# Zero matmuls moved to the front, memory rows copied by DMA, a different reuse order of two PSUM banks and function tables loaded by name, in an attention and MoE kernel

## The chip, the cores and the metric

The kernel runs on one core of a Trainium2 chip. The metric is the device time in microseconds (us) of one execution. Three executions of the kernel before were timed; their median is 242.94 us (241.69 to 244.8). A further execution was profiled, and the views quoted here are of that one.

The engines go by the names of the profile: PE multiplies matrices (PEld is its weight load), DVE and ACT are the vector and scalar engines, POOL is GpSimd, SP issues transfers. POOL and SP each have a queue of transfers.

## The reference

Chunked attention with a few memory rows, then a two-layer MLP with a sine-based activation. Inputs are float32: q, k and v of (4, 8, 768, 64), memory keys and values of (4, 8, 8, 64), `w_in` of (512, 2048), `w_out` of (2048, 512), `alpha` of (2048).

```python
chunk, left_ctx, right_ctx = (32, 16, 8)
for c in range(nc):
    l_start, r_end = max(0, c*32 - 16), min(S, c*32 + 32 + 8)
    k_full = concatenate([mem_k, k[:, :, l_start:r_end]])     # 8 memory rows first
    v_full = concatenate([mem_v, v[:, :, l_start:r_end]])
    a = softmax(q_chunk @ k_full.T / sqrt(D))
    out[chunk] = a @ v_full
x = out as (3072 tokens, 512)
h = x @ w_in
g = h + sin(alpha * h)**2 / alpha
result = g @ w_out
```

## The kernel before, in words

The four batches (768 tokens each) go through attention one after the other, and each then through the MLP. All data is cast to bfloat16 on its way in, and PE adds up in float32 in PSUM. The order of the instructions on each engine is the order in which the Python code issues them; nothing is reordered.

**Attention.** A batch is cut into 8 query blocks of 96 rows (`NJ`, `QW`). A block's keys are 128 wide: the context and, in the middle, the 8 memory rows. For the first batch the work goes by pairs of heads (`attention_first`): `turn` (L214) transposes k and q of a pair of heads on PE, `put_k` (L226) and `put_q` (L239) copy them out of PSUM on ACT and DVE, `unit_scores` (L309) multiplies and exponentiates, `unit_values` (L334) multiplies with the values tile `vw` and divides by the sum, and `unit_turn` (L354) transposes the result into `xT`. For the later batches `scores` (L249), `values` (L274) and `turn_x` (L294) do the same for each block. Keys and queries of batches 2 and 3 are gathered as rows into `kst` and `qst` by DMAs on POOL's queue (`load_rows`, L134) and transposed by DMAs on SP's queue (`cross`, L156).

**Memory rows.** The 8 memory values of a batch have to stand in partitions 64 to 71 of `vw`, once for each head and block: `put_memv` (L180) copies them there from the chip tile `memv_st`, on DVE for batches 0 and 1 and on POOL for batches 2 and 3. The memory keys of batches 2 and 3 are copied by POOL into `kst` in `load_rows` (L147); those of batches 0 and 1 are transposed by PE (L545) and put in their place by DVE (`put_memk`, L186).

**MLP.** `layer` (L575) goes over 16 tiles of the hidden width. For each, `first` (L456) does 8 matmuls (L442) into one of three or four two-bank pieces of PSUM, ACT takes the sine (L462), ACT, DVE or POOL squares it (L466, L469), and DVE adds h and writes `gT` (L472), which frees the PSUM piece. The second matmul (`second`, L479) is a generator: one call of it gives one matmul (L485) with 512 columns. Its 6 times 16 matmuls are fed in between the work of the next batch's attention and next layer (`feed.take`). After each 16 the result is copied to `o_sb` (L494 on DVE or L496 on ACT, by turns) and stored from SP's queue.

**The two single banks.** Banks 6 and 7 (ring `one`) are shared by `second`, which keeps one for 16 matmuls, and by `turn_x`, which uses the other for a few transposes. `take_bank` (L87) gives the first bank of the ring that nobody keeps and moves it to the ring's end.

**The start.** PE multiplies zeros (`warm`, L304, tile `idle`) in a few places where it would otherwise wait. ACT's table of functions is loaded when the kernel goes over from `Exp` to `Sin` or back; `preload_act_table` does it where the code says, otherwise it happens just ahead of the first instruction that needs the other table.

Of the kernel before, what the change touches and what calls it, by code (L numbers as in the profile page):

```python
# [15 lines left out]
ACTF = mybir.ActivationFunctionType  # L16
# [26 lines left out]
def kernel(  # L43
# [90 lines left out]
    def load_rows(b):  # L134
        for j in range(NJ):
            lo = QW * j - 16
            r0 = max(0, -lo)
            nc.gpsimd.dma_start(  # L138
                kst[r0:64, j, :].rearrange("p (h d) -> p h d", d=D),
                k[b, :, lo + r0:lo + 64, :].rearrange("h p d -> p h d"),  # L140
            )
            n = min(56, S - (QW * j + 48))
            nc.gpsimd.dma_start(  # L143
                kst[72:72 + n, j, :].rearrange("p (h d) -> p h d", d=D),
                k[b, :, QW * j + 48:QW * j + 48 + n, :].rearrange("h p d -> p h d"),
            )
        nc.gpsimd.tensor_copy(  # L147
            kst[64:72], memk_st[64:72, b - 2, :].unsqueeze(1).to_broadcast([NM, NJ, H * D])
        )
        for t in range(NSUB):  # L150
            nc.gpsimd.dma_start(  # L151
                qst[:, t, :].rearrange("p (h d) -> p h d", d=D),
                q[b, :, P * t:P * t + P, :].rearrange("h p d -> p h d"),
            )
# [25 lines left out]
    def put_memv(b, eng, h0, h1):  # L180
        eng.tensor_copy(  # L181
            vws[b % 2][64:72, h0:h1, :, 0:D],
            memv_st[64:72, b, h0:h1, :].unsqueeze(2).to_broadcast([NM, h1 - h0, NJ, D]),
        )

    def put_memk(b):  # L186
        nc.vector.tensor_copy(
# [166 lines left out]
    def unit_turn(xT, hp, half, x_blk):  # L354
# [7 lines left out]
        )  # L362

    def attention_first(kq, early, ahead):
        xT = xp.tile([P, KT, S], BF, name="xT")
        pt, xb = {}, {}

        def turns(hp):
            put_k(0, hp, turn(kq[0], hp, None))
            put_q(0, hp, turn(kq[1], hp, None))  # L370

        def sc(hp):
            for half in range(2):
                pt[hp, half] = unit_scores(hp, half)

        def pv(*u):
            xb[u] = unit_values(*u, pt[u])

        def x(*u):
            unit_turn(xT, *u, xb.pop(u))  # L380

        warm(12)
        turns(0)
        warm(1)
        turns(1)
        sc(0)
        turns(2)
        sc(1)
        turns(3)
        sc(2)  # L390
        sc(3)
        nc.scalar.preload_act_table(ACTF.Sin)
        early()
        warm(10)
        plan(big=rings["t"][0:1] + rings["big"])
        pv(0, 0)
        pv(0, 1)
        warm(1)
        x(0, 0)
        pv(1, 0)  # L400
        warm(1)
        x(0, 1)
        pv(1, 1)
        warm(1)
        x(1, 0)
        warm(4)
        x(1, 1)
        pv(2, 0)
        pv(3, 0)
        warm(1)  # L410
        x(2, 0)
        pv(2, 1)
        warm(1)
        x(3, 0)
        pv(3, 1)
        ahead(0, 0, xT)
        x(2, 1)
        ahead(1, 0, xT)
        x(3, 1)
        ahead(2, 0, xT)  # L420
        return xT

    def attention(b, stream, shares, lag):
        xT = xp.tile([P, KT, S], BF, name="xT")
        ptl, xbl = {}, {}
        for s in range(NJ + lag + 1):
            n = shares[s] if s < len(shares) else 0
            if s < NJ:
                ptl[s] = scores(b, s)
            stream.take(n // 2)  # L430
            if 0 <= s - lag < NJ:
                xbl[s - lag] = values(b, s - lag, ptl.pop(s - lag))
            stream.take(n - n // 2)
            if 0 <= s - lag - 1 < NJ:
                turn_x(xT, s - lag - 1, xbl.pop(s - lag - 1))
        return xT
# [42 lines left out]
    def second(i, gT):  # L479
        for s in range(NSUB):  # L480
            bank = take_bank("one")
            kept.add(bank)
            o = ps[:, bank, :]
            for ft in range(FT):
                nc.tensor.matmul(  # L485
                    o, gT[:, ft, P * s:P * s + P], w_out_sb[:, ft, :],
                    start=(ft == 0), stop=(ft == FT - 1),
                )
                if ft < FT - 1:
                    yield  # L490
            kept.remove(bank)
            o_sb = mlp.tile([P, d_model], F32, name="o_sb", bufs=2)
            if s % 2 == 0:
                nc.vector.tensor_copy(o_sb[:], o)  # L494
            else:
                nc.scalar.copy(o_sb[:], o)  # L496
            nc.sync.dma_start(out[S * i + P * s:S * i + P * s + P, :], o_sb[:])
            yield
# [7 lines left out]
        nc.sync.dma_start(memk_f[NM * bb:NM * bb + NM], mem_k[bb].rearrange("h n d -> n h d"))  # L506
    nc.sync.dma_start(alpha_rows[:], moe_alpha.rearrange("(ft p) -> ft p", p=P))
    nc.vector.memset(idle[:], 0.0)
    for vw in vws:
        nc.vector.memset(vw[0:32, 0, 0, 0:D], 0.0)  # L510
        nc.vector.memset(vw[96:128, H - 1, NJ - 1, 0:D], 0.0)
# [28 lines left out]
    nc.vector.tensor_copy(biasb[:, 0, 0, 0:1], biasm[:, 3:4])  # L540
    nc.vector.tensor_copy(biasb[:, 1, 3, 2:3], biasm[:, 4:5])
    nc.vector.tensor_copy(memk_bf[:], memk_f[0:32])
    mt = packed(single(), HP, 32)
    for g in range(HP):
        nc.tensor.transpose(mt[:, g, :], memk_bf[0:32, 2 * g:2 * g + 2, :].rearrange("p e d -> p (e d)"), ident[0:32, 0:32])  # L545
    nc.vector.tensor_copy(memkT[:], mt)
    put_memk(0)
    nc.vector.tensor_copy(ident_f[:], ident[0:FT, 0:FT])
    for pt in pts:
        nc.vector.memset(pt[:, H * QW:H * QW + 32], 0.0)  # L550
# [5 lines left out]
    def early():  # L556
        at = single()[:, 0:FT]
        nc.tensor.transpose(at, alpha_rows[:], ident_f[:])
        nc.vector.tensor_copy(alpha_sb[:], at)
        nc.vector.reciprocal(inv_alpha[:], alpha_sb[:])  # L560
        put_memv(0, nc.vector, 0, H)
        put_memv(1, nc.vector, 0, H)

    feed = Feed()
    xT = attention_first(kq, early, ahead)
# [39 lines left out]
    for bb in range(2):  # L605
        nc.gpsimd.dma_start(memk_st[64:72].rearrange("n b (h d) -> n b h d", d=D)[:, bb],
                            mem_k[2 + bb].rearrange("h n d -> n h d"))
    feed.take(8)
    prs = [pair_up(kq1[n % 2], n // 2) for n in range(3)]
    for pc in range(2 * HP):  # L610
# [2 lines left out]
        if pc + 3 < 2 * HP:  # L613
            prs.append(pair_up(kq1[(pc + 3) % 2], (pc + 3) // 2))
        feed.take(2)
    put_memk(1)
    load_rows(2)
    xT = attention(1, feed, (6, 4, 4, 3, 3, 3, 3, 3, 3, 3, 3), 2)
    load_v(2, 0, H)
    put_memv(2, nc.gpsimd, 0, H)  # L620

    for i in range(1, B):
        last = i == B - 1

        def begin(ft, i=i):
            if ft == 2 and i + 1 < B:
                cross(i + 1)

        plan(h=rings["big"])
        layer(i, xT, "AAAV", begin, feed.left() - (0 if last else 16))  # L630
        if not last:
            if i + 2 < B:
                load_rows(i + 2)
            plan(big=rings["h"])
            xT = attention(i + 1, feed, (10, 8, 4, 4, 3, 3, 3, 3, 4, 4, 4), 2)
            if i + 2 < B:
                load_v(i + 2, 0, H)
                put_memv(i + 2, nc.gpsimd, 0, H)
    feed.take(200)


# [28 lines left out]
```

## Time and profile before

| | us |
|---|---|
| median of three executions | 242.94 |
| the profiled execution's own time | 242.81 |
| its span, first to last instruction | 241.0 |
| PE busy | 212.7 |
| ACT busy | 153.2 |
| DVE busy | 141.7 |
| POOL busy | 96.2 |

The profiled execution's time lies within 0.13 us of the median; 1.8 us of it lie outside the span. The stages by time in the span: start and first attention to about 34, first layer to about 57, second attention to about 83, second layer to about 110, third attention to about 131, third layer to about 161, fourth attention to about 181, fourth layer to about 215, and then PE alone with the rest of the last second matmul.

In the timeline, a row gives the start, the busy time, engine, line and operation, and in brackets how long the engine had been idle before it and what ended that. In the view of waits, a row gives who waited for whom, the total in us, how often, and the longest.

### The profile page before, as it was taken

Reading aid. Unit: us, or ns where it says so; the run is one execution under the profiler, and the core shown is the slowest. Engines: PE = TensorE matmul, PEld = TensorE weight load, DVE = VectorE, ACT = ScalarE, POOL = GpSimd, SP = SyncE. Lnnn points to the kernel's source line nnn. Section 1 sums busy time; section 2 is a strip of 40 time slices with the busy share of each in tenths; the row PEclk is TensorE's granted clock in tenths of the full one; section 3 lists DMA queues with packets and bytes.
Section 4 is the critical chain, followed back from the end, with each engine's and each line's share of the span. In section 5 each row is a group of like instructions: output and inputs, shape, how many; then the busy total and the mean of one; then the engine's idle time right before and its main releaser. Section 6 shows DMA issues by size and latency. Waiting matters only on the chain.

```text
span 241.0 us, 4411 instructions
## 1 busy us (share of the span) xinstructions
PE 212.7 (88%) x1707; PEld 117.0 (49%) x1733; DVE 141.7 (59%) x246; ACT 153.2 (64%) x224; POOL 96.2 (40%) x106
## 2 busy tenths in 40 slices
PE   0989787898989997999778999999789899999993
PEld 0454454555445554554445555554455455554441
DVE  5155756898828648778675476645673646663110
ACT  2069349689387497899663977898647577680000
POOL 8867603497999992599991000000000000000000
PEclk9999999999999999999999999999999999999998
DMA  6999999999999999999999954302001101102212
GB/s 89 166 122 121 205 207 207 204 139 89 78 94 117 115 124 131 128 175 149 189 125 136 133 109 88 109 3 87 31 15 46 44 0 44 45 4 87 87 44 87
DMA packets 90646, 25.14 MB, mean 104 GB/s; under 512 B 78833, under 2 KB 87553, under 8 KB 90625
## 3 DMA queue, kind: packets, MB, share of 16 engines
q0 software_dynamic: 71616, 14.82, 110.7%
q1 hardware_dynamic: 19008, 10.04, 20.3%
q8 instruction: 13, 0.21, 0.4%
q14 instruction: 9, 0.07, 0.1%
HBM read 29.67 MB, written 6.29 MB: 149 GB/s over the span
## 4 chain that ended last, share of the span: by engine, by line
PE 64%; DVE 15%; ACT 9%; issue 9%; POOL 1%; DVEq 0%; ACTq 0%; POOLq 0%
PE ps L485 28%; PE ps L442 24%; DVE gT L472 5%; ACT u L462 4%; PE ps L254 3%; DVE u L469 3%; PE ps L307 2%; PE ps L280 2%; ACT u L466 2%; DVE o_sb L494 1%; PE ps L297 1%; PE ps L218 1%; DVE x_blk L347 1%; DVE qT L240 1%; DVE vw L181 1%
## 5 line engine op out<-in xcount | busy, mean ns | idle before, releaser
L485 PE MATMUL ps<-w_out_sb,gT 128*128 128x512 bf16 x360 | 96.8, 379 | 4.1 <-ACT o_sb L496 1.4
L442 PE MATMUL ps<-xT,w_in_sb 128*128 128x384 bf16 x512 | 92.3, 326 | 5.0 <-DVE gT L472 4.8
L472 DVE SCALAR_TENSOR_TENSOR gT<-u,inv_alpha,ps 128x768 bf16<-128x768 f32 x64 | 63.7, 1012 | 34.9 <-ACT u L466 33.8
L462 ACT ACTIVATE u<-ps,alpha_sb 128x768 f32<-128x768 f32 x64 | 57.1, 898 | 24.1 <-PE ps L442 23.3
L442 PEld LDWEIGHTS <-w_in_sb 128*128 128x128 bf16 x512 | 49.6, 98 | 43.9 <-issue 8.7
L485 PEld LDWEIGHTS <-gT 128*128 128x128 bf16 x384 | 34.3, 98 | 31.5 <-issue 2.6
L466 ACT ACTIVATE u<-u 128x768 f32<-128x768 f32 x44 | 37.1, 844 | 1.3
L267 ACT ACTIVATE pt<-ps,biasm 128x256 bf16<-128x256 f32 x72 | 28.6, 480 | 9.2 <-PE ps L254 9.0
L496 ACT COPY o_sb<-ps 128x512 f32<-128x512 f32 x12 | 7.0, 586 | 25.2 <-PE ps L485 19.2
L494 DVE COPY o_sb<-ps 128x512 f32<-128x512 f32 x12 | 8.3, 689 | 21.7 <-PE ps L485 21.7
L469 DVE TENSOR_TENSOR u<-u 128x768 f32<-128x768 f32 x16 | 19.7, 1231 | 2.2 <-ACT u L462 2.1
L287 DVE TENSOR_TENSOR x_blk<-ps,rinv 96x512 bf16<-96x512 f32 x24 | 16.5, 686 | 0.8
L228 ACT COPY kT<-ps 128x672 bf16<-128x672 bf16 x8 | 5.7, 717 | 14.1 <-PE ps L221 10.7
L138 POOL DMA_DIRECT2D kst<-in_k_dram x16 | 11.3, 704 | 7.6 <-DMA kT<-kst 7.6
L286 DVE RECIPROCAL rinv<-ps 96x8 f32<-96x8 f32 x24 | 4.9, 202 | 13.4 <-PE ps L280 13.4
L469 POOL TENSOR_TENSOR u<-u 128x768 f32<-128x768 f32 x4 | 6.4, 1606 | 14.8 <-ACT u L462 14.7
L143 POOL DMA_DIRECT2D kst<-in_k_dram x16 | 11.8, 736 | 0.1
L297 PEld LDWEIGHTS <-x_blk 96*128 96x128 bf16 x96 | 6.7, 97 | 8.9 <-issue 3.4
L280 PEld LDWEIGHTS <-pt 128*128 128x128 bf16 x192 | 9.0, 97 | 4.1 <-issue 0.3
L300 DVE COPY xT<-ps 128x384 bf16<-128x384 bf16 x24 | 8.3, 347 | 3.8 <-PE ps L297 3.8
L151 POOL DMA_DIRECT2D qst<-in_q_dram x12 | 10.5, 906 | 0.0
L297 PE MATMUL ps<-ident,x_blk 96*128 96x96 bf16 x96 | 8.0, 205 | 2.6 <-DVE o_sb L494 2.5
(75 smaller groups left out, 175.7 us busy)
## 6 DMA issues: line engine op xcount, KB each, us to landing
out_dram<-o_sb SPq DMA_DIRECT2D x24, 256.0 KB, 2.0
vw<-in_v_dram POOLq DMA_DIRECT2D x6, 384.0 KB, 10.7
w_out_sb<-in_moe_w_out_dram POOLq DMA_DIRECT2D x2, 1024.0 KB, 18.2
w_in_sb<-in_moe_w_in_dram POOLq DMA_DIRECT2D x3, 512.0 KB, 12.2
qst<-in_q_dram POOLq DMA_DIRECT2D x12, 128.0 KB, 5.0
kst<-in_k_dram POOLq DMA_DIRECT2D x14, 64.0 KB, 4.3
kst<-in_k_dram POOLq DMA_DIRECT2D x14, 56.0 KB, 4.7
k_bf<-in_k_dram POOLq DMA_DIRECT2D x4, 192.0 KB, 5.7
```

What stands on the lines that cost most here:

```text
L138: nc.gpsimd.dma_start(kst[r0:64, j, :].rearrange("p (h d) -> p h d", d=D), k[b, :, lo + r0:lo + 64, :].rearrange("h p d -> p h d"),)
L143: nc.gpsimd.dma_start(kst[72:72 + n, j, :].rearrange("p (h d) -> p h d", d=D), k[b, :, QW * j + 48:QW * j + 48 + n, :].rearrange("h p d -> ...
L267: nc.scalar.activation(pt[:, 0:H * QW].rearrange("p (g e c) -> p g e c", g=2, e=4)[:, :, :, 32 * m:32 * m + 32], sc[:, :, 0:4 * QW].rearra ...
L280: nc.tensor.matmul(otv[:, e, hp, :], pt[:, QW * i:QW * i + P], vws[b % 2][:, 2 * hp + e, j, 0:D + 1],)
L287: nc.vector.tensor_tensor(out=x_blk[:].rearrange("p g e d -> p e g d"), in0=otv[0:QW, :, :, 0:D], in1=rinv[:].unsqueeze(3).to_broadcast([Q ...
L297: nc.tensor.transpose(xtp[:, kt, :], x_blk[:, kt].rearrange("p e d -> p (e d)"), ident[0:QW, 0:QW])
L442: nc.tensor.matmul(hT[:, hf, 0:HALF], w_in_sb[:, kt, P * ft:P * ft + P], xT[:, kt, HALF * hf:HALF * hf + HALF], start=(kt == 0), stop=(kt ...
L462: nc.scalar.activation(u[:], hT[:, :, 0:HALF], ACTF.Sin, scale=alpha_sb[:, ft:ft + 1])
L466: nc.scalar.activation(u[:], u[:], ACTF.Square)
L469: eng.tensor_tensor(out=u[:], in0=u[:], in1=u[:], op=ALU.mult)
L472: nc.vector.scalar_tensor_tensor(out=gT[:, ft, :].rearrange("p (e c) -> p e c", e=2), in0=u[:], scalar=inv_alpha[:, ft:ft + 1], in1=hT[:, ...
L485: nc.tensor.matmul(o, gT[:, ft, P * s:P * s + P], w_out_sb[:, ft, :], start=(ft == 0), stop=(ft == FT - 1),)
```

## The change

Five edits, whose line numbers in the changed kernel are a little higher.

1. **Start.** 8 zero matmuls are issued right behind the memset of the zeros. The transposes of the first batch's memory keys, with their two DVE copies, move from the front of PE's order to behind the first pair of heads. The 12 zero matmuls ahead of the first pair of heads go; between the first and the second there are 2 instead of 1.
2. **Memory rows.** In `load_rows`, and for the values of batches 1, 2 and 3, the copies on POOL and DVE become DMAs from the chip tiles on SP's queue: one for the keys, and 8 (one for each block) for the values of a batch.
3. **Banks.** When `second` gives up its bank, the bank goes to the end of the ring.
4. **Tables.** The loads are asked for by name: `Sin` behind the last `Exp` of an attention, `Exp` behind the last piece of k of batch 1 and behind each later layer.
5. `put_memk(1)` is issued ahead of the second batch's transposes rather than behind them.

```diff
@@ load_rows
-        nc.gpsimd.tensor_copy(
+        nc.sync.dma_start(
             kst[64:72], memk_st[64:72, b - 2, :].unsqueeze(1).to_broadcast([NM, NJ, H * D])
         )
@@ behind put_memv
+    def send_memv(b):
+        for j in range(NJ):
+            nc.sync.dma_start(vws[b % 2][64:72, :, j, 0:D], memv_st[64:72, b])
@@ attention_first
-        warm(12)
         turns(0)
-        warm(1)
+        mt = packed(single(), HP, 32)
+        for g in range(HP):
+            nc.tensor.transpose(mt[:, g, :], memk_bf[0:32, 2 * g:2 * g + 2, :].rearrange("p e d -> p (e d)"), ident[0:32, 0:32])
+        nc.vector.tensor_copy(memkT[:], mt)
+        put_memk(0)
+        warm(2)
         turns(1)
         sc(0)
@@ attention
                 ptl[s] = scores(b, s)
+            if s == NJ - 1:
+                nc.scalar.preload_act_table(ACTF.Sin)
             stream.take(n // 2)
@@ second
             kept.remove(bank)
+            rings["one"].remove(bank)
+            rings["one"].append(bank)
             o_sb = mlp.tile([P, d_model], F32, name="o_sb", bufs=2)
@@ the start
     nc.vector.memset(idle[:], 0.0)
+    warm(8)
     for vw in vws:
...
     nc.vector.tensor_copy(memk_bf[:], memk_f[0:32])
-    mt = packed(single(), HP, 32)
-    for g in range(HP):
-        nc.tensor.transpose(mt[:, g, :], memk_bf[0:32, 2 * g:2 * g + 2, :].rearrange("p e d -> p (e d)"), ident[0:32, 0:32])
-    nc.vector.tensor_copy(memkT[:], mt)
-    put_memk(0)
     nc.vector.tensor_copy(ident_f[:], ident[0:FT, 0:FT])
@@ early
         put_memv(0, nc.vector, 0, H)
-        put_memv(1, nc.vector, 0, H)
+        send_memv(1)
@@ between the first layer and the second attention
+    put_memk(1)
     feed.take(8)
...
         feed.take(2)
-    put_memk(1)
+        if pc == 2 * HP - 2:
+            nc.scalar.preload_act_table(ACTF.Exp)
     load_rows(2)
     xT = attention(1, feed, (6, 4, 4, 3, 3, 3, 3, 3, 3, 3, 3), 2)
     load_v(2, 0, H)
-    put_memv(2, nc.gpsimd, 0, H)
+    send_memv(2)
@@ the loop over the later batches
             plan(big=rings["h"])
+            nc.scalar.preload_act_table(ACTF.Exp)
             xT = attention(i + 1, feed, (10, 8, 4, 4, 3, 3, 3, 3, 4, 4, 4), 2)
             if i + 2 < B:
                 load_v(i + 2, 0, H)
-                put_memv(i + 2, nc.gpsimd, 0, H)
+                send_memv(i + 2)
```

PE's first instructions, before: `memk_bf` holds the memory keys, `idle` the zeros, `k_bf` the first pair of heads. Repetitions are left out.

```order
L545 LDWEIGHTS memk_bf
L545 MATMUL ps<-ident,memk_bf 128x32
...
L307 LDWEIGHTS idle
L307 MATMUL ps<-idle 128x512
...
L221 LDWEIGHTS k_bf
L221 MATMUL ps<-ident,k_bf 64x128
```

PE's first instructions in the changed kernel, where the zeros are L311, the transposes of k and q L225 and those of the memory keys L389.

```order
L311 LDWEIGHTS idle
L311 MATMUL ps<-idle 128x512
...
L225 LDWEIGHTS k_bf
L225 MATMUL ps<-ident,k_bf 64x128
...
L225 LDWEIGHTS q_bf
L225 MATMUL ps<-ident,q_bf 64x128
...
L389 LDWEIGHTS memk_bf
L389 MATMUL ps<-ident,memk_bf 128x32
```

The zeros now come first and the memory keys behind the first pair of heads.

DVE at the end of the first batch's scores, before and in the changed kernel: `alpha_sb` is what the sine needs, `vw` the values tiles, `rinv` the first step behind the values' matmul.

```order
L559 COPY alpha_sb<-ps 128x16
L560 RECIPROCAL inv_alpha<-alpha_sb 128x16
L181 COPY vw_87<-memv_st 8x64x64
L181 COPY vw_88<-memv_st 8x64x64
L346 RECIPROCAL rinv<-ps 96x8
```

```order
L567 COPY alpha_sb<-ps 128x16
L568 RECIPROCAL inv_alpha<-alpha_sb 128x16
L181 COPY vw_87<-memv_st 8x64x64
L350 RECIPROCAL rinv<-ps 96x8
```

One of the two copies of memory values ahead of the first `rinv` has left DVE.

SP's queue, the difference in its first part: `out_dram` are the stores of results.

```order
-L497 DMA out_dram<-o_sb 128x512 x4
+L188 DMA vw_88<-memv_st 8x8x64 x8
+L509 DMA out_dram<-o_sb 128x512
+L147 DMA kst<-memk_st 8x8x512
+L509 DMA out_dram<-o_sb 128x512 x2
+L188 DMA vw_87<-memv_st 8x8x64 x8
+L509 DMA out_dram<-o_sb 128x512
 L158 DMA_TRANSPOSE kT_83<-kst 128x4x128 x8
```

The transfers of memory rows now stand between the stores and ahead of the transposes of batch 2; POOL's copies L147 and L181 are gone from its order.

## The prediction

> **What bounds the kernel now.** I read the view of PE's waits first, since the table above gives PE as the busiest engine by far, and then the timeline at each place that the waits name. PE's waits, with their totals:
>
> ```profile
> PE ps L545 <- DVE memk_bf L542: 5.9, 1, 5.9
> PE ps L442 <- DVE gT L472: 4.8, 7, 1.6
> PE ps L297 <- DVE o_sb L494: 2.5, 2, 1.2
> ...
> PE ps L485 <- ACT o_sb L496: 1.4, 2, 0.7
> PE ps L254 <- DVE gT L472: 1.4, 1, 1.4
> PE ps L485 <- DVE o_sb L494: 1.3, 2, 0.8
> PE ps L254 <- DVE kT L187: 1.0, 1, 1.0
> ```
>
> The last stage is PE alone and the change does not touch its work. What it can win is in these rows: the start, in which PE stands until the memory keys are there; waits for the copy of a result out of a single bank (2.5, 1.4 and 1.3, together 5.2); and waits for `gT`, of which two have a cause that the change removes. A wait of PE in the middle of the kernel counts in full as long as PE finds other work late too, and between about 67 and 215 us PE rarely waits for anything else.
>
> **The start.** Timeline of the first 30 us:
>
> ```profile
> 0.86 0.27 DVE L508 MEMSET idle<- 128x256 uint32 x1 [0.86 <-PEq L654]
> ...
> 6.07 5.08 PE L307 MATMUL ps<-idle 128*128 128x512 bf16 x12
> ...
> 11.08 0.53 PE L221 MATMUL ps<-ident,k_bf 128*64 128x128 bf16 x12
> ...
> 13.58 0.93 POOL L173 DMA_DIRECT2D vw<-in_v_dram  x1 [0.66 <-DMA q_bf<-in_q_dram]
> ...
> 14.92 1.52 ACT L328 ACTIVATE pt<-ps 128x768 bf16<-128x768 f32 x2 [0.77 <-PE ps L320]
> ...
> 16.33 0.71 ACT L228 COPY kT<-ps 128x672 bf16<-128x672 bf16 x1
> ...
> 17.08 0.32 DVE L234 COPY kT<-ps 128x48 bf16<-128x48 bf16 x2 [1.71 <-ACT kT L228]
> 17.32 0.95 DVE L240 COPY qT<-ps 128x768 bf16<-128x768 bf16 x1
> ...
> 20.87 0.34 PE L320 MATMUL ps<-qT,kT 64*128 64x96 bf16 x8
> 21.58 0.34 PE L320 MATMUL ps<-qT,kT 64*128 64x96 bf16 x8
> ...
> 22.24 2.11 PE L307 MATMUL ps<-idle 128*128 128x512 bf16 x9 [0.16 <-issue]
> 22.61 2.55 DVE L181 COPY vw<-memv_st 8x4096 bf16<-8x4096 bf16 x2
> 24.18 0.67 PE L340 MATMUL ps<-vw,pt 128*128 128x65 bf16 x16
> 25.19 0.20 DVE L346 RECIPROCAL rinv<-ps 96x8 f32<-96x8 f32 x1
> ```
>
> Before, the first pair of heads is transposed at 11.08, behind twelve zero matmuls that began only at 6.07. In the changed kernel the zeros can begin at 1.2 and end by 4.6 (8 by 5.08/12 = 0.42), and the pair is then taken when it lands. I do not credit the 5 us in full, because the transfers end later: POOL's row at 13.58 is a queue slot that came free when the third piece of q had landed, so that piece is there at about 13.5 and no edit makes it earlier. From there the chain is, each step from the rows above: transposes 0.53 (14.1), the second pair's scores, the first half of them 21.58 - 20.87 = 0.71 (14.8), two exponentials 1.52 (16.3), `put_k` of the last pair on ACT 0.71 (17.05), DVE's two small copies until L240 starts 0.24 and L240 0.95 (18.3), L320 of the last pair 0.34 and its second half 0.71 (19.4). Before, that end is 21.58 + 0.34 = 21.9. The start gives 2.5, not 5.
>
> Behind it stand ten zeros and L340, before at 24.18 and now at 21.7. `rinv` then waited until 25.16 for the second of the two copies in the L181 row (2.55 for both); without it, it follows L340 by 0.45, at 22.15. Together 25.19 - 22.15 = **3.0**.
>
> The cover of this is the second half of v, which the later units need:
>
> ```profile
> 16.23 0.68 POOL L178 DMA_DIRECT2D vw<-in_v_dram  x1
> ...
> 29.49 0.67 PE L340 MATMUL ps<-vw,pt 128*128 128x65 bf16 x16
> ```
> ```profile
> vw<-in_v_dram POOLq DMA_DIRECT2D x1, 31.0 KB, 8.8
> ```
>
> It lands at 16.23 + 8.8 = 25.0 and is now needed at 29.49 - 3.0 = 26.5: 1.5 us are left, so the gain passes on.
>
> The zeros serve the clock. Twelve of them ran at 0.42 each, and later ones at 2.11/9 = 0.23, so PE began at half speed and was at full speed for the transposes at 11.08. Eight end earlier than twelve did: whether they suffice no row shows. If not, PE's terms in that chain (0.53 + 0.71 + 0.34 + 0.71 = 2.3) double, until the dense stretch from 13.5 on releases the clock. I put that loss at 1.6; its bounds are 0, and 2.3 + 10 x (0.42 - 0.23) = 4.2 if the ten zeros behind the scores are slow too. The Trainium skill's page "TensorE: Matmul & The Clock Gate", Part 1, says that the clock is released after a busy window of about 3.4 us which runs freely, and its table "Why this matters for your kernels" asks for at least 4 us of work without a pause. By that rule 8 zeros, 3.4 us, would as a rule not fill a window, and it speaks against this edit; the row of twelve agrees, whose 5.08 us passed nearly whole at half speed.
>
> **Memory rows.** POOL's copies, DVE's squares beside them, and PE:
>
> ```profile
> 88.16 3.59 POOL L181 COPY vw<-memv_st 8x4096 bf16<-8x4096 bf16 x1
> ...
> 90.62 1.95 DVE L469 TENSOR_TENSOR u<-u 128x768 f32<-128x768 f32 x1
> ...
> 93.74 2.98 PE L442 MATMUL ps<-xT,w_in_sb 128*128 128x384 bf16 x16 [1.31 <-DVE gT L472]
> ...
> 110.58 3.59 POOL L147 COPY kst<-memk_st 8x4096 bf16<-8x4096 bf16 x1
> ...
> 111.65 3.33 DVE L469 TENSOR_TENSOR u<-u 128x768 f32<-128x768 f32 x1
> ...
> 116.08 0.35 PE L254 MATMUL ps<-qT,kT 64*128 64x96 bf16 x8 [1.35 <-DVE gT L472]
> ```
> ```profile
> L469 DVE TENSOR_TENSOR u<-u x16: 950/958/3329, 40.5 to 216.4; 128x768 f32<-128x768 f32 x16
> ```
>
> A square takes 0.96 (median of 16). The two long ones end with POOL's copy or after it: 88.16 + 3.59 = 91.75, and 110.58 + 3.59 = 114.17. DVE stood still for POOL, 1.0 and 2.4 us, and PE behind it 1.31 and 1.35. With the copies gone PE gets back 1.0 at the first (DVE's own loss bounds it) and 1.35 at the second (PE's wait bounds it): **2.4**, and at most 2.7. That POOL is freed of 14.4 us of copies is worth nothing beside that: no row has PE wait for POOL.
>
> What comes instead: 24 transfers for the values and 2 for the keys, on SP, between stores. SP has no other work, and a store behind them delays only the reuse of `o_sb`, of which there are two, with one result each 7 us or so. The price is in the transfer engines, where the first 8 run beside the loads of v and `w_in`. They are 8 x 8 x 8 = 512 packets of 128 bytes. What a packet costs, from the queues over the first 20 us (q1, SP's) and over the whole span (q0, POOL's):
>
> ```profile
> q1 hardware_dynamic: 320, 0.07, 2.0%
> ```
> ```profile
> q0 software_dynamic: 71616, 14.82, 110.7%
> ```
>
> That is 0.020 x 16 x 20 us / 320 = 20 ns and 1.107 x 16 x 241 us / 71616 = 60 ns: 10 to 31 us of one engine's time. Spread over 8 engines it is 1.3 to 3.8 us on each, on 16 half of that. I take it as hidden by the 1.5 us of slack (20 ns, the same queue); the bound above is 3.8 - 1.5 = 2.3. The Trainium skill's page "DMA: Bandwidth & Descriptors", Rules for kernel authors, says that a slowest dimension below 16 confines a transfer to as many engines; these have 8 partitions, so by it the 8-engine figure holds. No run here shows it yet.
>
> **Banks.** Where PE waits for a bank that was just given up:
>
> ```profile
> 77.38 0.59 PE L485 MATMUL ps<-w_out_sb,gT 128*128 128x512 bf16 x2 [0.54 <-DVE o_sb L494]
> ...
> 122.53 0.68 DVE L494 COPY o_sb<-ps 128x512 f32<-128x512 f32 x1
> ...
> 123.26 0.33 PE L297 MATMUL ps<-ident,x_blk 96*128 96x96 bf16 x4 [1.25 <-DVE o_sb L494]
> ...
> 123.80 0.39 PE L485 MATMUL ps<-w_out_sb,gT 128*128 128x512 bf16 x1
> ...
> 130.19 0.59 PE L485 MATMUL ps<-w_out_sb,gT 128*128 128x512 bf16 x2 [0.72 <-ACT o_sb L496]
> ...
> 190.13 0.38 PE L485 MATMUL ps<-w_out_sb,gT 128*128 128x512 bf16 x1 [0.78 <-DVE o_sb L494]
> ```
>
> The waits view counts those of 1.25 and 0.72 twice (third and fourth attention). In the changed ring the next taker gets the other bank. At 77.38 and 190.13 that one is free: 0.5 and 0.8. At 123.26 `turn_x` gets the free bank at 122.0, but the L485 behind it (123.80) then needs the bank in question at 122.55, whose copy ends at 122.53 + 0.68 = 123.2: 0.7 of the 1.25 comes back, 0.55 is won, twice. At 130.19 the other bank is `turn_x`'s own, read until about 129.7: 0.45 is won, twice. Sum 0.5 + 0.8 + 1.1 + 0.9 = **3.3**, of 5.2 at most.
>
> **The rest.**
>
> ```profile
> 66.72 0.22 DVE L187 COPY kT<-memkT 128x256 bf16<-128x256 bf16 x1
> ```
>
> This copy stands between PE and the second batch's first scores (the wait of 1.0); moved ahead it gives **0.2**, since the copy of q before it stays. The named table loads stand in the same gaps of ACT, where no row has PE wait for a load: nothing. Were one on the path, it would cost its 1.28.
>
> **Sum.** 3.0 + 2.4 + 3.3 + 0.2 = 8.9. The profiled execution took 242.81, the median of the runs is 242.94, so no correction: 242.8 - 8.9 = **233.9**.
>
> **Rivals.**
> - *The zeros don't release the clock.* For it: eight are fewer than the twelve that hardly sufficed; against it: the transposes and scores that follow keep PE busy too. 233.9 + 1.6 = 235.5.
> - *The bank waits only move.* The copy out of the bank takes as long as ever, and there are two banks; if whoever comes second waits in full, the 3.3 goes: 237.2. Against it: at 77.38 and 190.13 the next taker has no one close behind.
> - *The transfers' slack is too short.* At 60 ns a packet on 8 engines the second half of v comes 3.8 later: 233.9 + 2.3 = 236.2.
> - *Slower: the packets queue on one engine.* 31 us there ahead of v's last piece, less 1.5 of slack, stall PE for 29 us: 233.9 + 29 = 263. It makes the kernel slower from 8.9 + 1.5 = 10.4 us on, some 170 packets at 60 ns on one engine. Against it: each of these transfers writes 8 partitions in 64 separate packets, and nothing in the rows of q1 hints at a pile-up.
>
> **Chances.** Forecast 0.50, clock 0.28, banks 0.10, short slack 0.08, slower 0.04. Low end: all 5.2 of the banks and 2.7 of the squares, 233.9 - 1.9 - 0.3 = 231.7, rounded to 231.5 for the start's unknowns. High end: the clock case with its upper bound, 233.9 + 4.2 = 238.1, and the bank case, 237.2; I take 238.0. A measurement of this kernel can tell about 2% from no change, which is 4.9 us or 238.1: all cases but the last lie below it, some of them only by a little. Faster 0.86, within 2% 0.10, slower 0.04.
>
> **What would show it.** The first transposes of k before 7 us and L340's first at about 21.7 would bear out the start; the spacing of L320's halves (0.7 or 1.4) decides on the clock. No square above 1.1 us bears out the memory rows. Bank waits of PE for `o_sb` should sum to about 2, not 5.2. The prediction is wrong if the values' matmul of the later units waits for a transfer, or if layers that were paced by PE turn out to be paced by ACT, so that regained time comes back as another wait.

## The result, and the profile after

| | before | after |
|---|---|---|
| median of four executions, us | 242.45 (241.69 to 244.8) | 233.26 (233.11 to 233.95) |
| the profiled execution, us | 242.81 | 233.11 |
| its span, us | 241.0 | 231.3 |
| PE / DVE / POOL busy, us | 212.7 / 141.7 / 96.2 | 215.7 / 136.4 / 80.8 |

The ratio is 0.9611, with a 95% interval of 0.954 to 0.9681: 9.2 us less, where 8.9 were predicted. All 9.7 us of the span are found by setting the two timelines beside each other at marks that both have (the first `rinv`, PE's first scores and first layer matmul of each batch, and the end of the last layer's matmuls). For the second batch after the change the mark is 63.03, where seven of the first eight scores run behind a wait of 0.65, and not 62.16, where one ran alone:

| stretch | before | after | won |
|---|---|---|---|
| start to the first `rinv` | 25.19 | 20.89 | 4.30 |
| rest of the first attention | 7.07 | 7.07 | 0 |
| first layer and the transposes of the second batch | 34.74 | 35.07 | -0.33 |
| second attention | 15.70 | 15.05 | 0.65 |
| second layer | 27.32 | 26.32 | 1.00 |
| third attention | 20.77 | 18.64 | 2.13 |
| third layer | 30.82 | 30.85 | -0.03 |
| fourth attention | 19.36 | 18.39 | 0.97 |
| fourth layer | 34.26 | 33.35 | 0.91 |
| PE alone to the end | 25.77 | 25.67 | 0.10 |

PE's waits after the change (who waited for whom, total in us, how often, longest):

```profile
PE ps L452 <- DVE gT L482: 3.9, 8, 1.6
PE ps L495 <- DVE o_sb L506: 1.6, 2, 0.8
...
PE ps L311 <- DVE vw L523: 1.2, 1, 1.2
PE ps L258 <- DVE qT L244: 0.7, 1, 0.7
```

The wait of 5.9 for the memory keys is gone and the waits for `o_sb` went from 5.2 to 1.6. The wait of 1.2 at L311 is new, but it is only the time until the first tiles are set, with which the kernel begins.

**The start**, timeline of the changed kernel:

```profile
1.19 3.59 PE L311 MATMUL ps<-idle 128*128 128x512 bf16 x8 [1.19 <-DVE vw L523]
5.23 0.85 PE L225 MATMUL ps<-ident,k_bf 128*64 128x128 bf16 x12 [0.45 <-DMA k_bf<-in_k_dram]
...
8.19 0.85 PE L225 MATMUL ps<-ident,k_bf 128*64 128x128 bf16 x12
...
11.15 0.53 PE L225 MATMUL ps<-ident,k_bf 128*64 128x128 bf16 x12
...
12.06 0.93 POOL L173 DMA_DIRECT2D vw<-in_v_dram  x1 [0.38 <-DMA q_bf<-in_q_dram]
...
14.57 0.53 PE L225 MATMUL ps<-ident,q_bf 128*64 128x128 bf16 x12 [0.35 <-DMA q_bf<-in_q_dram]
...
15.50 0.95 DVE L244 COPY qT<-ps 128x768 bf16<-128x768 bf16 x1
...
18.27 2.33 PE L311 MATMUL ps<-idle 128*128 128x512 bf16 x10
18.87 1.22 DVE L181 COPY vw<-memv_st 8x4096 bf16<-8x4096 bf16 x1
20.44 0.67 PE L344 MATMUL ps<-vw,pt 128*128 128x65 bf16 x16
20.89 0.20 DVE L350 RECIPROCAL rinv<-ps 96x8 f32<-96x8 f32 x1 [0.81 <-PE ps L344]
```

Three things are to be seen. The first pair is transposed at 5.23, before the 7 us that the prediction gave as a sign. It takes 0.85 and not 0.53, so in this execution the eight zeros had not released the clock; the transposes at 11.15 are the first at full speed. And POOL's row that marks the third piece of q stands at 12.06, not 13.58. L344 comes at 20.44, 1.3 earlier than the 21.7 of the prediction.

**The squares**, timeline, and the view of the tile `u` (shortest/median/longest in ns):

```profile
85.99 0.95 DVE L479 TENSOR_TENSOR u<-u 128x768 f32<-128x768 f32 x1
...
88.12 1.46 PE L452 MATMUL ps<-xT,w_in_sb 128*128 128x384 bf16 x8 [0.31 <-DVE gT L482]
...
106.03 0.95 DVE L479 TENSOR_TENSOR u<-u 128x768 f32<-128x768 f32 x1
```
```profile
L479 DVE TENSOR_TENSOR u<-u x16: 950/952/1543, 36.2 to 206.8; 128x768 f32<-128x768 f32 x16
```

Both long squares are back at 0.95. The longest left, 1.54, is the one in the first layer that had that length before as well, beside a square of POOL's.

**The bank**, timeline:

```profile
116.22 0.38 PE L495 MATMUL ps<-w_out_sb,gT 128*128 128x512 bf16 x1 [0.80 <-DVE o_sb L506]
...
165.72 0.38 PE L495 MATMUL ps<-w_out_sb,gT 128*128 128x512 bf16 x1 [0.80 <-DVE o_sb L506]
```

These two are all that is left of PE's waits for `o_sb`: the matmul behind `turn_x` takes the bank whose copy is not yet made.

### The profile page after: what moved, and what is told of

Read it like the earlier page. It is cut to its first block, busy times and chain, and to the rows that moved or that the text cites. A ratio compares the mean times of both kernels' runs of the same rounds, so it can differ in the third digit from the quotient of the medians.

```text
span 231.3 us, 4462 instructions
## 1 busy us (share of the span) xinstructions
PE 215.7 (93%) x1730; PEld 117.5 (51%) x1730; DVE 136.4 (59%) x245; ACT 153.3 (66%) x224; POOL 80.8 (35%) x102
## 4 chain that ended last, share of the span: by engine, by line
PE 67%; DVE 11%; ACT 9%; issue 6%; DMA 3%; POOL 2%; DVEq 0%; ACTq 0%; POOLq 0%
PE ps L495 32%; PE ps L452 25%; ACT u L472 5%; DVE gT L482 4%; DMA q_bf<-in_q_dram 3%; PE ps L258 3%; ACT u L476 2%; PE ps L284 2%; PE ps L301 1%; PE ps L311 1%; DVE x_blk L291 1%; DVE x_blk L351 1%; POOL k_bf L164 1%; PE ps L222 1%; POOL q_bf L164 1%
## 5 line engine op out<-in xcount | busy, mean ns | idle before, releaser
L495 PE MATMUL ps<-w_out_sb,gT 128*128 128x512 bf16 x384 | 102.1, 380 | 2.2 <-DVE o_sb L506 1.6
L479 DVE TENSOR_TENSOR u<-u 128x768 f32<-128x768 f32 x16 | 15.9, 995 | 2.2 <-ACT u L472 2.1
L138 POOL DMA_DIRECT2D kst<-in_k_dram x16 | 11.0, 688 | 12.6 <-DMA kT<-kst 12.6
L143 POOL DMA_DIRECT2D kst<-in_k_dram x16 | 11.5, 719 | 0.5 <-DMA vw<-in_v_dram 0.5
L151 POOL DMA_DIRECT2D qst<-in_q_dram x12 | 10.5, 902 | 2.0 <-DMA qT<-qst 1.5
L311 PE MATMUL ps<-idle 128*128 128x512 bf16 x29 | 9.9, 465 | 1.2 <-DVE vw L523 1.2
```

The costliest lines, as they stand in the source:

```text
L138: nc.gpsimd.dma_start(kst[r0:64, j, :].rearrange("p (h d) -> p h d", d=D), k[b, :, lo + r0:lo + 64, :].rearrange("h p d -> p h d"),)
L143: nc.gpsimd.dma_start(kst[72:72 + n, j, :].rearrange("p (h d) -> p h d", d=D), k[b, :, QW * j + 48:QW * j + 48 + n, :].rearrange("h p d -> ...
L311: nc.tensor.matmul(z, idle[:, 0:P], idle[:])
L479: eng.tensor_tensor(out=u[:], in0=u[:], in1=u[:], op=ALU.mult)
L495: nc.tensor.matmul(o, gT[:, ft, P * s:P * s + P], w_out_sb[:, ft, :], start=(ft == 0), stop=(ft == FT - 1),)
```

## The experiments

Twelve kernels ran, each beside runs of the kernel before on the same chip. Each edit is against the changed kernel.

| run | median, us (range) | ratio to before (95%) |
|---|---|---|
| `e1_start_old` | 236.37 (236.01 to 236.72) | 0.9745 (0.9681 to 0.9809) |
| `e4_pool_rows` | 237.12 (235.49 to 237.8) | 0.9766 (0.9693 to 0.984) |
| `e5_spare_copy` | 235.52 (234.58 to 237.77) | 0.9724 (0.9643 to 0.9804) |
| `e6_banks_old` | 237.72 (235.8 to 238.54) | 0.9776 (0.9685 to 0.9866) |
| `a1_after` | 233.32 (232.13 to 233.79) | 0.9621 (0.9557 to 0.9686) |
| `e2_no_zeros` | 233.4 (232.98 to 235.32) | 0.9648 (0.9576 to 0.9719) |
| `e3_zeros_16` | 233.28 (232.02 to 234.47) | 0.9626 (0.9557 to 0.9696) |
| `e12_memv1_pool` | 233.22 (232.44 to 234.73) | 0.9627 (0.9543 to 0.9711) |
| `e7_memv1_dve` | 233.04 (232.94 to 233.69) | 0.9615 (0.9552 to 0.9677) |
| `e8_tables_memk_old` | 233.29 (232.62 to 234.32) | 0.963 (0.9569 to 0.9691) |
| `e10_swap_evac` | 232.93 (232.5 to 234.86) | 0.9627 (0.9561 to 0.9693) |
| `e15_mid_swap` | 231.78 (231.47 to 232.97) | 0.9583 (0.9548 to 0.9619) |

The first four ran on one chip, the next four on a second, then three on the first again and the last on a third. No unaltered run stands beside the first four, but all their executions (234.58 at least) lie above all eight of the changed kernel (233.95 at most). One execution of a kernel differs from another by 0.7 to 3.5 us, so an effect below 1 us is read from the stretches of the profile, not from the medians.

### The start undone

```diff
-    warm(8)
...
+    mt = packed(single(), HP, 32)
+    for g in range(HP):
+        nc.tensor.transpose(mt[:, g, :], ...)
+    nc.vector.tensor_copy(memkT[:], mt)
+    put_memk(0)
...
+        warm(12)
         turns(0)
-        mt = packed(single(), HP, 32)
...
-        put_memk(0)
-        warm(2)
+        warm(1)
```

> The changed kernel with the old start: twelve zero matmuls behind the memory keys, everything else as changed. Theory of the chain (the start is bound by the landing of the third pieces of k and q, then by exponentials, put_k and L244): the start's gain goes except for the 0.55 of the copy that has left DVE, so 3 to 4 us come back, 236.5 to 237.5. Rival, the start is hidden by the transfers of v and w_in: no more than 1 us, 234.3. Of the landing: the slot that the third piece of q frees stood at 13.6 before and 12.1 after. If the order of PE's work had a hand in that, it stands at about 13.6 here; if it is chance from run to run, it can stand anywhere between, and differs among the runs that have the new start.

The first `rinv` stood at 24.16, 3.27 later than in the changed kernel, and the run took 3.1 more (236.37 against 233.26). PE's waits show what is back:

```profile
PE ps L553 <- DVE memk_bf L550: 5.9, 1, 5.9
```

Timeline of this run:

```profile
6.07 4.61 PE L311 MATMUL ps<-idle 128*128 128x512 bf16 x12
10.61 0.53 PE L225 MATMUL ps<-ident,k_bf 128*64 128x128 bf16 x12
...
23.71 0.67 PE L344 MATMUL ps<-vw,pt 128*128 128x65 bf16 x16
...
24.16 0.20 DVE L350 RECIPROCAL rinv<-ps 96x8 f32<-96x8 f32 x1 [0.80 <-PE ps L344]
```

So the order at the start is worth about 3.1 to 3.3 (the median lies just below the 236.5 to 237.5 expected). The other 1.03 of the 4.30, between 24.16 here and 25.19 before, are two things. The twelve zeros took 4.61 here and 5.08 before, so all that follows them, from the first pair (10.61, 11.08) to the values' matmul (23.71, 24.18), comes 0.47 earlier. And `rinv` follows that matmul by 0.45 here and by 1.01 before, where DVE had two copies to make: 0.56 for the copy that has left DVE. The landing of the third piece of q has no part in it: its POOL row stands at 11.95 here and at 13.58 before, and PE's rows from the first pair on keep the same distances. So 13.58 was the landing in one execution, no property of the kernel.

### Memory rows of batches 2 and 3 by POOL again

```diff
-        nc.sync.dma_start(
+        nc.gpsimd.tensor_copy(
             kst[64:72], ...
...
-    send_memv(2)
+    put_memv(2, nc.gpsimd, 0, H)
...
-                send_memv(i + 2)
+                put_memv(i + 2, nc.gpsimd, 0, H)
```

> The changed kernel with the memory rows of batches 2 and 3 copied by POOL again (values and keys). Theory (DVE's square stands still while POOL copies): one square in the second layer and one at its end lengthen to 2 to 3.4 us again, PE waits behind them, 2.4 us come back: 235.7. Rival (POOL's copies were off the path and the gain there had another cause): 233.3.

```profile
84.87 3.59 POOL L181 COPY vw<-memv_st 8x4096 bf16<-8x4096 bf16 x1
...
86.41 2.87 DVE L479 TENSOR_TENSOR u<-u 128x768 f32<-128x768 f32 x1
...
90.44 1.84 PE L452 MATMUL ps<-xT,w_in_sb 128*128 128x384 bf16 x9 [2.22 <-DVE gT L482]
```

POOL's copy ends at 88.46, and the square, begun at 86.41, at 89.28: it got its usual 0.8 to 0.95 only once POOL was done. PE waits 2.22 behind it and 1.25 behind the second one (3.23, beside the copy of the keys at 107.18). The second layer takes 28.23 in place of 26.32 and the third attention 19.96 in place of 18.64: 3.2 in all, at the two places that the prediction named and at no other. It is more than the 2.4 won, and the median lies 1.4 above the 235.7 expected, since the first copy now begins earlier against its square: the square starts 1.54 into the copy, and 2.46 before.

### The same copying by POOL into a tile that nobody reads

```diff
+    def spare_copy():
+        for n in (5, 3):
+            nc.gpsimd.tensor_copy(spare[64:72, ...], memv_st[64:72, 0]...)
...
+        spare_copy()
         for t in range(NSUB):
...
+    spare_copy()
```

The memory rows still go by DMA; POOL only copies as many bytes again at the same places.

> The changed kernel with extra copies on POOL at the places of the old ones, of the same rows, in two pieces (8x2560 and 8x1536), into a spare tile that nobody reads. If DVE stands still because POOL is copying, the squares lengthen as in the run with the old copies and 1 to 2.4 us come back (234.5 to 235.7). If it was the data (somebody waiting for the rows), nothing changes: 233.3.

```profile
84.78 4.45 POOL L160 COPY spare<-memv_st 8x2560 bf16<-8x2560 bf16 x2
...
85.89 2.01 DVE L488 TENSOR_TENSOR u<-u 128x768 f32<-128x768 f32 x1
...
89.07 2.98 PE L461 MATMUL ps<-xT,w_in_sb 128*128 128x384 bf16 x16 [1.37 <-DVE gT L491]
```

The square is long again (2.01) beside a copy whose result nobody waits for, and the second layer takes 27.89 in place of 26.32. The second square, at 106.99, took 0.95, because POOL reached its copy only at 108.37. So it is POOL's copying itself that holds DVE, not the data.

`e12_memv1_pool` (below) shows the limit of this: its POOL copy covers DVE's `x_blk`, which reads PSUM and the small `rinv`, and that keeps its usual 0.69:

```profile
29.11 3.59 POOL L181 COPY vw<-memv_st 8x4096 bf16<-8x4096 bf16 x1
29.30 0.69 DVE L351 TENSOR_TENSOR x_blk<-ps,rinv 96x512 bf16<-96x512 f32 x1
```

The Trainium skill's page "SBUF — State Buffer", section "Who interferes with whom", says that a DVE instruction with two inputs in SBUF contends with a GpSimd instruction that reads SBUF, and that one with at most one such input does not, outside its two-port modes. Both pairs of rows agree with it.

### The bank order undone

```diff
-            rings["one"].remove(bank)
-            rings["one"].append(bank)
```

> The changed kernel without the two lines that put a given-up bank last. Theory: PE's waits for o_sb stand at 5.2 us again instead of 1.6 plus 0.6, and 3.3 us come back: 236.6. Rival (the waits only move, the time is the same): 233.3.

PE's waits:

```profile
PE ps L301 <- DVE o_sb L504: 2.5, 2, 1.3
PE ps L344 <- DMA vw<-in_v_dram: 2.4, 2, 1.5
PE ps L495 <- ACT o_sb L506: 1.7, 2, 1.0
...
PE ps L495 <- DVE o_sb L504: 1.3, 2, 0.8
```

The waits for `o_sb` are back at 5.5. Against the unaltered changed kernel the second, third and fourth attention and the fourth layer lose 0.43, 0.99, 0.96 and 0.92, in all 3.3. The span (236.7) is 5.4 longer than in the profile after, and the median 1.1 above the 236.6 expected; the other 2.1 lie at the start, where PE waited 2.4 for v, and where no result has been copied yet.

### Unaltered, without the zeros, and with sixteen

```diff
-    warm(8)
```
for `e2_no_zeros`, and `warm(16)` in its place for `e3_zeros_16`; `a1_after` has no edit.

> The changed kernel once more, unaltered, as the measure for the runs beside it and to see how much one execution differs from another. Both theories: 233.3 to 235.5 us. The theory that the landing of v's second half has a slack of about 1.5 us and overruns it in some executions expects runs of up to 2 us above the fastest, and a wait of PE at L344 for vw in the profile if it falls on such a one; the rival, that the executions differ only by noise everywhere, expects the runs within 0.5 us of each other.

> The changed kernel without its 8 zero matmuls at the front; all else as changed. Theory: the clock's release at about 10 us came from the dense row of transposes and scores from 5.2 us on, not from the zeros, which had ended at 4.8 and after which the transposes still took 0.85 us each; so without them the transposes begin at about 5.2, run at half speed to about 10 as before, and rinv stands at 20.9, plus or minus 0.4; the time is the changed kernel's, plus or minus 0.7. Rival: the zeros carry part of the window; then the release comes later by up to 3.5 us, L344's first matmuls, the scores and the ten zeros behind them run at half speed, rinv comes 1.0 to 2.5 us later and the time is that much longer.

> The changed kernel with 16 zero matmuls at the front in place of 8. They run to about 8 us at half speed, so the first pair of heads is transposed at about 8 in place of 5.2. Theory: the chain that sets rinv starts at the landing of the third piece of q, 12 to 13.5 us, so the pairs before it have time to spare: the clock is released before 8, the first two pairs then run at 0.53 in place of 0.85, and rinv stands at 20.9 plus or minus 0.5, the time within 0.7 of the changed kernel's. Rival: the chain hangs on PE's own start; then rinv comes up to 2.8 us later and the time with it.

The medians are 233.32, 233.4 and 233.28: neither the eight zeros nor eight more do anything that can be measured. Timeline without them:

```profile
5.36 0.85 PE L225 MATMUL ps<-ident,k_bf 128*64 128x128 bf16 x12 [5.36 <-DMA k_bf<-in_k_dram]
...
8.32 0.85 PE L225 MATMUL ps<-ident,k_bf 128*64 128x128 bf16 x12
...
11.51 0.53 PE L225 MATMUL ps<-ident,k_bf 128*64 128x128 bf16 x12
...
20.20 0.67 PE L344 MATMUL ps<-vw,pt 128*128 128x65 bf16 x16
```

The first two pairs run at half speed, and the third is in time for the chain. `rinv` stands at 20.65, earlier than in the profile after. With sixteen zeros the first pair starts at 6.40 at full speed, and `rinv` stood at 22.65: 1.25 later than I allowed, yet not by the rival's way, since PE then waited 1.73 at 10.44 for the second piece of q, and the clock was taken back behind that wait (last section). The time is what the theory said, the place of `rinv` is not.

`a1_after` spreads over 1.7 us and so contradicts the rival's 0.5. But its profile, of its longest execution, has no wait for v at all; PE waited 1.4 for q in it, and `rinv` stood at 22.08. So the theory had the wrong transfer for that execution. The clock had a part too:

```profile
9.29 0.85 PE L225 MATMUL ps<-ident,q_bf 128*64 128x128 bf16 x12 [0.60 <-DMA q_bf<-in_q_dram]
...
12.45 0.85 PE L225 MATMUL ps<-ident,k_bf 128*64 128x128 bf16 x12
...
21.63 0.67 PE L344 MATMUL ps<-vw,pt 128*128 128x65 bf16 x16
```

Behind the row at 9.29 PE waited for no transfer, and it ran at half speed until about 14. From there to L344 it took 12.34, while the same work took 10.55 in `e1_start_old` (13.16 to 23.71) at full speed: half speed made PE's way to the first `rinv` 1.8 longer here.

### Memory values of batch 1 by DVE, and by POOL

```diff
-        send_memv(1)
+        put_memv(1, nc.vector, 0, H)
```

is `e7_memv1_dve`; in `e12_memv1_pool` the line becomes `put_memv(1, nc.gpsimd, 0, H)` behind `load_qk(1, kq1, 0, H)`.

> The changed kernel, but DVE copies the memory values of batch 1 again, behind those of batch 0, and the 8 transfers on SP's queue at 15 us go. Theory, the prediction's second term of the start: the one copy left ends at about 20.1 in the changed kernel; a second of 1.2 to 1.3 us behind it ends at 21.4, the first rinv waits for it and comes 0.5 us later than L344 alone would allow (which is L344's first start plus 0.45), and the time is 0.3 to 0.6 longer than the changed kernel's. Rival: the transfers beside the loads of v delay it, so taking them away wins as much as the copy loses; then PE never waits for vw at L344 and the time is the changed kernel's or up to 0.5 less.

> The changed kernel, but the memory values of batch 1 are copied by POOL, behind its last loads at about 30 us, where POOL has nothing else, in place of the 8 small transfers on SP's queue at 15 us. Theory that these transfers cost nothing as long as v lands in time: the same time as the changed kernel plus or minus 0.5, but in executions where v's second half is late it is less late, so the median is lower by up to 1 and the runs lie closer together. Rival, that POOL's copy at 30 us meets a square or a copy of DVE's and holds it up as in the layers: one square or copy of DVE's takes 2 to 3 us, and the time is 0.5 to 1.5 longer.

Neither differs from the changed kernel, and the runs with POOL's copy do not lie closer together (2.3 us). Timeline of the one with DVE:

```profile
18.36 2.55 DVE L181 COPY vw<-memv_st 8x4096 bf16<-8x4096 bf16 x2
```
```profile
21.29 0.67 PE L344 MATMUL ps<-vw,pt 128*128 128x65 bf16 x16 [1.20 <-DMA vw<-in_v_dram]
```

The two copies end at 20.91, before L344 starts, because L344 waited for the first half of v. So my theory of 0.3 to 0.6 fell: the copy lies beside that wait. The rival fell too: with no small transfer on the way, PE still waited 1.20 for v, and 1.0 in the one with POOL, both times for its first half. Its last piece, 31.0 KB, took 10.5 and 10.9 us to land without the small transfers, and 9.7 and 10.1 with them (the profile after and `a1_after`). In seven of the twelve profiles with the changed start or a variant of it PE waits for v at L344, between 0.3 and 2.4 us in all; the small transfers are not needed for that.

### Tables and `put_memk(1)` as before

```diff
-            if s == NJ - 1:
-                nc.scalar.preload_act_table(ACTF.Sin)
...
-    put_memk(1)
     feed.take(8)
...
-        if pc == 2 * HP - 2:
-            nc.scalar.preload_act_table(ACTF.Exp)
+    put_memk(1)
     load_rows(2)
...
-            nc.scalar.preload_act_table(ACTF.Exp)
```

> The changed kernel with edits 4 and 5 undone: the function tables are loaded just ahead of the first instruction that needs them, as before, and put_memk(1) is issued behind the second batch's transposes. Theory, the prediction's: the loads stand in gaps of ACT, so only the copy of 0.22 us at L187 comes back to the path, ahead of the second batch's first scores: 0.2 longer at that place and nothing else, in all 0 to 0.3. Rival: the named loads are part of what was gained in the later stages; then each of the seven changes of table shows a load of about 1.3 us that PE waits for through a score or a gT, and the time is 1 us or more longer.

From the first transposes of the second batch to its first scores it takes 7.92 in place of 7.08 in `a1_after`, and the attention behind it 15.27 in place of 15.92, as a wait for `qT` of 0.6 is then covered: over both 23.19 in place of 23.00, so 0.2 lost, as the prediction had it. The third attention is 0.26 shorter. The median is 233.29. Edits 4 and 5 together are worth nothing that can be measured.

### Another engine for the copies to `o_sb`

```diff
-            if s % 2 == 0:
+            if s % 2 == 1:
                 nc.vector.tensor_copy(o_sb[:], o)
```

> The changed kernel, but the copies of the results to o_sb go by turns the other way round: ACT takes the even ones and DVE the odd ones. It tests whether the bank waits that are left (two of 0.8 us, at about 116 and 166 us, on a copy that DVE makes late because its own queue is full) come from the bank's order or from the engine that copies. Theory: the copy is late because DVE is busy with gT at that point; on ACT, which is less busy there, both waits go or shrink below 0.4, and the time is 0.6 to 1.6 less than the changed kernel's, if the odd results, now on DVE, are not waited for in their place. Rival: whoever copies, the bank comes free too late for a taker so close behind, and waits of the same total, 1.4 to 2, stand at the same or the neighbouring results; time within 0.4.

The waits at `turn_x`'s neighbour shrank from 0.80 to 0.33, twice, but the second attention got a wait of 0.71 for ACT's copy and the fourth layer one of 0.39 for `gT`. By stretches it won 1.2 and lost 1.2, and the median of 232.93 is within the rival's 0.4. So the engine does decide, place by place, and the last run kept only the places where the swap won:

```diff
-            if s % 2 == 0:
+            if (s % 2 == 0) != (3 <= NSUB * i + s < 15):
```

> The changed kernel with the copies to o_sb swapped between DVE and ACT only for the results 3 to 14 of the 24, counted through all batches. From the stages of the run with all of them swapped: against the unaltered changed kernel it took 0.35 less from the second layer's start to the third attention's, 0.55 less in the third attention and 0.3 less in the fourth, and gave back 0.6 in the second attention (a wait for ACT's copy of the third result) and 0.6 in the fourth layer and behind it. Theory: the engine that copies decides who waits for a bank, place by place, so the three gains stay and the two losses go: the stages named are 26.0, 18.1 and 18.1 us long, the second attention 15.9, the fourth layer and what follows 59.0; in all 1.2 less than the changed kernel, 232.1. Rival: the places hang together, so that what is won in one is waited for in the next; then a new wait of 0.3 to 0.7 for o_sb or gT stands in the third or fourth layer and the time is 232.8 to 233.4.

```profile
115.26 0.38 PE L495 MATMUL ps<-w_out_sb,gT 128*128 128x512 bf16 x1 [0.33 <-ACT o_sb L508]
...
164.16 0.38 PE L495 MATMUL ps<-w_out_sb,gT 128*128 128x512 bf16 x1 [0.33 <-ACT o_sb L508]
```

The second layer, third and fourth attention take 25.96, 18.08 and 18.08 (26.32, 18.64 and 18.39 before this edit); the second attention and the fourth layer lose nothing. That is 1.2 in the profile, and the median of 231.78 is 1.5 below that of the changed kernel: its highest of six (232.97) lies below the changed kernel's median in both of its sets of runs (233.26 and 233.32). These sets ran on other chips, and the intervals of the ratios to the kernel before overlap, so it is the stretches that show the 1.2. This is the best kernel of the study.

## Why the prediction was right

**The sum.** By the stretches of the table the gains are: start 4.30 - 0.33, squares 2.41 (1.00 in the second layer and 1.41 up to the third block's scores of the third attention), banks 3.25 (0.65, 0.72, 0.97 and 0.91; of the 0.65, 0.2 are rather L187's, since undoing the banks gives back 0.43 there), and 0.07 in the other stretches. Predicted were 3.0 + 0.2, 2.4, 3.3.

**The start, 3.0.** Its size is right on average: undoing it costs 3.1, and over the twelve profiles with the changed start or a variant of it `rinv` lies between 20.48 and 22.70, with a median of 21.75, 3.4 before 25.19 (predicted 22.15). Its working is right only in part, so that the size is partly luck. Right: the five us between 6.07 and 11.08 do not all come back, since the end of the chain hangs on transfers in the profile after. Wrong: that the third piece of q is there "at about 13.5 and no edit makes it earlier", and that the chain starts with it. POOL's row for it stands between 11.51 and 13.29 in the twelve profiles, and at 11.95 with the old order; a time read from one profile was taken for a bound. And in the profile after PE did not wait for that piece but for the last one, 0.35 at 14.57. Right only with the old order: 0.5 for the copy taken from DVE. It is 0.56 between the kernel before and `e1_start_old`, and nothing as long as v lands after it (`e7_memv1_dve`). As for the order itself, the zeros at the front bring nothing (`e2_no_zeros`), so that the memory keys, whose transposes no longer stand ahead of the first pair, and the twelve zeros that stood behind them, make up its gain. The two were not tried apart; in `e1_start_old` the zeros alone fill the time from 6.07 to 10.61.

**The clock.** The rival's premise held in the profile after, where the first two pairs ran at half speed. Its price of 1.6 did not show there: the first full-speed transposes came at 11.15, the halves of L324 stand 0.71 apart (the sign named for full speed), and PE had caught up by the last piece of q, for which it waited 0.35. Of the ten profiles with eight zeros at the front, the first transposes took 0.85 in two, 0.64 in one and 0.53 in seven. A price of that size did show in `a1_after`, up to 1.8, but in another way than the rival's: the clock had been released there and was taken back. The medians with no, eight and sixteen zeros show none of this.

**Short slack.** A values' matmul of the later units that waits for a transfer is what the prediction named as a sign that it is wrong. The profile after has no such wait; five of the twelve have one, of 0.22 to 1.49. So the slack of 1.5 is overrun in some executions, but the premise, the packets of the small transfers, is not borne out: v's last piece took no less time to land without them.

**Memory rows, 2.4.** Right at both places and by their bounds. Undoing it costs 3.2, since POOL's copy then meets the square at another moment. A price read from one overlap holds for that overlap.

**Banks, 3.3.** Right in sum: 3.25 won, 3.3 lost when undone, 1.6 left of waits where about 2 were predicted. The rival, that the waits only move, has a share: 0.80 stands at each of two places at which PE did not wait before; the sum had 0.7 there.

**The rest, 0.2.** The 0.2 for L187 is right in size, by `e8_tables_memk_old`, though it shows over the transposes and the attention behind them together. The profile after shows a loss of 0.33 up to the scores, which is another matter: POOL's copy of q waited for a load.

```profile
54.18 0.83 POOL L213 COPY pr<-q_bf 128x768 bf16<-128x768 bf16 x1 [2.80 <-DMA q_bf<-in_q_dram]
...
57.00 0.50 PE L222 MATMUL ps<-ident,pr 128*128 128x128 bf16 x6 [0.53 <-DVE kT L238]
```

In `a1_after` PE waited 0.2 at that place, so this too seems to be a landing of one execution; why it came late here was not tried.

## What to carry to other kernels

A wait in the middle of a chain is worth what stands behind it, and a landing time is a sample: before a chain is bounded by a transfer, look at more than one execution. Where two engines hold each other up, ask what each reads; where a buffer is waited for, ask whose queue its copy stands in, and choose the engine place by place. Warm-up work is worth its place only if the work that it speeds up is on the chain that ends last.

## What the runs showed of the hardware

The clock was taken back without any long pause. View of PE's busy time and granted clock (PEclk) by stretches of 3.4 us in the profile of `a1_after`; columns: stretch, length, PE busy with its instructions, PEclk, DMA share and GB/s:

```profile
4.40:7.80 3.40, 1.91 (x31) 0.94 1.25 171
7.80:11.20 3.40, 2.80 (x35) 0.50 1.10 153
11.20:14.60 3.40, 3.40 (x48) 0.56 2.04 167
14.60:18.00 3.40, 3.21 (x63) 1.00 4.47 106
```

PE was busy for 1.91 of 3.40 us, with no idle stretch above 0.76, and then ran at half speed for over 6 us, to about 14. With sixteen zeros it was busy for 1.47 in the stretch from 7.8 to 11.2, and the clock of the next one was 0.53. The Trainium skill's page "TensorE: Matmul & The Clock Gate", section "Why this matters for your kernels", gives pauses above about 3 us as what costs the clock in the middle of a kernel; here no pause came near that, and the clock was lost all the same. How much PE was busy does not settle it alone either. In the profile of `e10_swap_evac` PE was busy for less, with a pause of 1.84, and the clock stayed:

```profile
6.80:10.20 3.40, 1.56 (x30) 1.00 1.07 133
10.20:13.60 3.40, 2.91 (x57) 1.00 1.45 182
```

Whether it matters where such a stretch lies in time, or that much of this work is transposes, was not tried.

The loads by POOL's queue land at times that differ by some 2 us between profiles whose first loads are the same: the second piece of q was taken by PE at 8.7 to 10.5 us, the third had left its slot in the queue by 11.51 to 13.58, and L344 started between 20.0 and 22.3. That is where most of the spread between executions of one kernel seems to come from, together with the clock, since the third layer takes 30.83 to 30.85 us in all of these profiles; the runs that were only timed have no profile to show it.
